# Up products of the first 512 tokens as float16 pairs, and five plain float32 down blocks, in a fused attention and two-network kernel

## The chip, the core and the metric

One core of a Trainium2 chip runs the whole program. The metric is the device time of one launch in microseconds. The kernel before was timed three times; the median is the number to compare with.

## What is computed

```python
# q, k, v: 2 x 8 x 768 x 64; proj: 64 x 6
bucket(y) = sum over n of 2**n * (y @ proj > 0)[n]
scores = where(bucket(q) == bucket(k), q @ k.T / 8, -1e9)
attn = softmax(scores) @ v
x = attn, heads side by side           # 1536 tokens x 512
h = x @ w_in                           # 512 -> 2048
x = (h - tanh(h)) @ w_out              # 2048 -> 512
p = domain_probs / sum
out = sum over e of p[:, e] * (relu(x @ w1[e]) @ w2[e])   # 4 experts, 512 -> 1024 -> 512
```

The weights of the first network arrive as float64 and are turned into float32 on the chip.

## The kernel before

TensorE is fed numbers of few bits, so nearly every product is made three times, from a high and a low part of each factor: high by high, high by low, low by high. A part is float16 or, in some places, float32r (a float32 that TensorE reads rounded). Where an operand is split, ScalarE or VectorE writes the high part and VectorE or GpSimd writes the low part, the source less the high part. A plain float32 product needs no split.

The work in order: the attention of 16 heads (`weights`, `maxima`, `prep`), up to 241 us; the first network, up to about 480 us; the second network.

In the first network the tokens go in three chunks of 512 (c = 0, 1, 2) and the hidden units in 16 blocks of 128 (fb).

- Up products of chunk 0 (`network_up`): they run while heads of the second batch are still in the attention, because chunk 0 needs only the first batch. The chunk's transposed input `xp` lies in the space `xa`, a float32r pair of 2 x 512 words for each of four row blocks; the block's weights `wu` lie in `wp0`, split by `split`. Twelve products of 128x512 make a block (L329, in `up_steps`), issued in two pieces of UPN = 6. ScalarE then takes the tanh (L984), VectorE the difference (L985).
- The weights (`conv`): for each block the two halves of a float64 tile come by DMA into `raw`; VectorE shifts and masks (L791, L796), ScalarE scales the low words (L334), GpSimd adds (L799). i = 0 is the block of w_in, i = 1 that of w_out. The converted w_out block takes a place of the class `fo` or `fo2` (`out_of`).
- Chunks 1 and 2 go up together by seven products in place of eight (`moving1`, `up7`, `seven`): sums and differences of four transposed quarters are cut into float16 pairs `bx` (the tiles named `ab`), those of two w_in blocks into `ax` (the tiles `fc` and `xa`). Their products are L920.
- Down products (`network_down`): for chunk 0 the blocks in FULL = (0, 1, 2) are plain float32, four products of 128x512 each (L994, recorded as two each); the other blocks split `th` into `g` (the tiles `hp`) and w_out into `wd` (the tiles `wp`) as float32r pairs and run L316, 12 products a block.

Places: before, `fo` and `fo2` are empty during the attention. `switch` makes seven and three places when the attention's own tiles are released; six more `fo` places come from `xa` and `wp0` after the up products of chunk 0 (`after_c0`).

The order on every engine is fixed when the program is built. `Plan.order` walks a model clock; each operation has a priority p (low goes first), a cost, and one or several engines that may do it, and it starts when its inputs and a place for its output are ready. For float32r up pieces the model adds ENTRY when TensorE comes to them from something else. The table T holds the priorities: `up0` and `up` for the up products, `m1` for `moving1`, `d0` and `d0s` for the down blocks of chunk 0. The conversion of a w_out block has the priority of its down block less `c1`.

Of the kernel before, what the change touches and what calls it, by code (L numbers as in the profile page):

```python
# [7 lines left out]
F16 = mybir.dt.float16  # L8
F32 = mybir.dt.float32
F32R = mybir.dt.float32r  # L10
U32 = mybir.dt.uint32
AF = mybir.ActivationFunctionType
# [40 lines left out]
WSI, XSI = 64.0, 4.0  # L53
GR = 2
TAIL = 3
FULL = (0, 1, 2)
FULL_ROWS = 0.86
ENTRY = 0.15
UPN = 6
WHOLE = ((1,), ())  # L60
PV32 = 1.3
EXPO = 0x7F800000
# [1 line left out]
NRQ = 2  # L64
TE, AC, VE, GP, DM_Q = "TE", "AC", "VE", "GP", "DQ"
T = dict(
    lead=10.23, lag=4.92, ahead=7.54, cut=3.18, up0=57.54, up=3.1, pre=23.64, bits=14.11, val=10.87,
    near=0.06, wait=20.39, slow=0.64, near0=0.004, begin=16.219, dma=0.65, done=0.9, hold=0.33,
    st0=129.04, sb0=-110.12, turn=228.92, near2=0.0, hold2=0.16, slow2=0.58, st=49.91, sb=31.04, dl=53.23, gs=79.64, bs=40.55, ns=7.06, ta=15.94,
    u7=358.17, u7s=22.26, d0=204.19, d0s=20.59, d1=408.55, d1s=13.63, m1=204.38, few=16, rest=295.92, cut7=25.22, cut70=142.27, g=13.58, c1=6.0, keep=0.0, x2=706.74, p0=746.54,  # L70
)


# [41 lines left out]
class Plan:  # L115
# [140 lines left out]
def attn_moe_kernel(ctx: ExitStack, tc: tile.TileContext, qk, v, proj, ident, wa, wb, dp, out):  # L256
# [11 lines left out]
    def space(name, words, kind=F32):  # L268
        if name not in places:
            places[name] = pool(name, 1)  # L270
        return places[name].tile([P, words], kind, name=name)
# [3 lines left out]

    rw_t, tp_t = space("rw", 2 * 2 * CH, U32), space("tp", NTH * CH)
    hp_t, hp2_t = space("hp", 2 * 2 * CH, F32R), space("hp2", 4 * CH)
    xa_t, wu_t = space("xa", KB4 * 2 * CH, F32R), space("wp0", 2 * 2 * CH, F32R)

    id32 = cp.tile([P, P], F32, name="id32")  # L280
    id16 = cp.tile([P, P], F16, name="id16")
# [18 lines left out]
    def part(t, at, n):  # L300
        return t[:, at : at + n]

    def pairs(t, at, n):
        return [part(t, at + 2 * CH * i, 2 * CH).rearrange("p (a b) -> p a b", a=2) for i in range(n)]

    def singles(t, at, n):
        return [part(t, at + CH * i, CH) for i in range(n)]
# [39 lines left out]
    def banks(n, name, shape=(P, CH)):  # L347
# [19 lines left out]
        den=tiles(2, [P, NB, 1], F32, "den"),  # L367

        f=singles(fa_t, 0, 14) + singles(fa2_t, 0, 2),
        fo=[],  # L370
        fo2=[],
        raw=raws(rw_t),
        wu=pairs(wu_t, 0, 2),
        wd=[],

        xp=pairs(xa_t, 0, KB4),
        g=pairs(hp_t, 0, 2),
        th=singles(tp_t, 0, NTH),
        th0=singles(hp2_t, 0, 4),
# [394 lines left out]
    w1 = {}  # L774

    def out_of(fb):
        return ("fo2" if fb < 3 else "fo", fb)

    def conv(fb, i, p):

# [21 lines left out]
    def split(p, dst, src, r, w, use=(), psum=False, gp=True, after=()):  # L802

        hi, lo = (lambda: dst()[:, 0, :]), (lambda: dst()[:, 1, :])
        how = {AC: (0.48 if psum else 0.52, act_copy(hi, src))}
        if not psum:
            how[VE] = (0.34, lambda: nc.vector.tensor_copy(hi(), src()))
        first = add(p, how, r, [(w, "hi")], use, port=not psum, after=after)
        h32 = lambda: hi().bitcast(F32)
        how = {VE: (0.6, sub(nc.vector, lo, src, h32))}  # L810
        if gp and not psum:
            how[GP] = (1.23, sub(nc.gpsimd, lo, src, h32))
        add(p + 0.1, how, [*r, (w, "hi")], [(w, "lo")], use, port=not psum)
        begun[w] = first
        return [(w, "hi"), (w, "lo")]
# [17 lines left out]
    def make_xT(c, kb, p):  # L833

        t = ("xp", c, kb)
        pt = turned(c, kb, p, [t])
        split(p + 0.1, lambda: pl[t], lambda: pl[pt], [pt], ("xT", c, kb), [t], psum=True)

    def scaled(p, hi, lo, src, by, n, r, k, use, psum=False):
        add(p, {AC: (0.05 + n * 0.92e-3, act_copy(hi, src, scale=by))}, r, [(k, "hi")], use)  # L840
# [128 lines left out]
    def network_up(c, fb, p, cut):  # L969

        w, ph, th = ("wu", c, fb), ("up", c, fb), th_of(c, fb)
        ks = split(p - cut, lambda: pl[w], lambda: pl["f", fb], [("f", fb)], ("w", c, fb, 0), [w])
        steps = {}

        def step(m):
            if not m:
                steps.update(enumerate(up_steps(pl[ph], pl[w], [pl["xp", c, kb] for kb in range(KB4)])))
            steps[m]()

        for m in range(0, 3 * KB4, UPN):  # L980
            add(p, {TE: (0.227 * UPN, lambda m=m: [step(m + i) for i in range(UPN)])},
                ks + [(("xT", c, kb), i) for kb in range(KB4) for i in ("hi", "lo")], [ph],
                [w] + [("xp", c, kb) for kb in range(KB4)], run="up")
        add(p + 0.5, {AC: (0.48, lambda: nc.scalar.activation(pl[th], pl[ph], AF.Tanh, scale=1.0 / XSI))}, [ph], [th])  # L984
        add(p + 0.6, {VE: (0.6, lambda: nc.vector.scalar_tensor_tensor(  # L985
            out=pl[th], in0=pl[ph], scalar=1.0 / XSI, in1=pl[th], op0=ALU.mult, op1=ALU.subtract
        ))}, [ph, th], [th])

    def network_down(c, fb, p, cut):
# [404 lines left out]
    for fb in range(NF1):  # L1394
        conv(fb, 0, up_at(fb) - T["ahead"])
    for fb in range(NF1):
        conv(fb, 1, down_at(0, fb) - T["c1"])
    for fb in range(NF1):
        network_up(0, fb, up_at(fb), T["cut"])
    moving1(T["m1"])  # L1400
# [117 lines left out]
    c0 = those("xp", "wu")  # L1518

    def after_c0():  # L1520
        t = late["xa"] = space("xa", 8 * CH)
        late.update(ax=sevens(t, 0), fo=singles(t, 7 * CH // 2, 4))
        t = space("wp0", 4 * CH)
        late["sx"] = quads(t, 0)
        late["fo"] += singles(t, 2 * CH, 2)
        return late["fo"]

    gives_later("fo", 6, after_c0, c0)
    gives_later("ax", 1, lambda: late["ax"], c0)
    gives_later("wr", 2, lambda: made["th1"], those("th1"))  # L1530
    gives_later("sx", 1, lambda: late["sx"], c0)
    gives_later("g", 2, lambda: pairs(space("hp2", 4 * CH, F32R), 0, 2), those("th0"))
# [107 lines left out]
```

## Time and profile before

| what | before |
|---|---|
| median of 3 runs | 914.13 us (913.98 to 917.42) |
| the profiled execution | 916.71 us |
| its span, first to last instruction | 914.9 us |
| TensorE (PE) busy | 893.8 us, 98% |
| VectorE (DVE) busy | 799.5 us, 87% |
| ScalarE (ACT) busy | 630.9 us, 69% |
| GpSimd (POOL) busy | 428.0 us, 47% |
| mean granted TensorE clock | 0.994 |

Busy time is the time in which at least one instruction of the engine is in flight. Matmuls overlap, so the spacing of their starts, not their duration, says what one costs.

### The profile page before, as it was taken

How to read it: one execution, taken by the hardware profiler on the slowest of the kernel's cores; microseconds unless marked ns; L12 is line 12 of the kernel's file. 1: busy time of each engine (PE TensorE's matmuls, PEld its weight loads, DVE VectorE, ACT ScalarE, POOL GpSimd, SP SyncE). 2: the span in 40 equal slices, each digit the busy share in tenths (PEclk: the TensorE clock that was granted, in tenths of full speed). 3: DMA queues.
4: the chain of work that ended last, by engine and by line, in shares of the span. 5: the costliest groups of instructions: out<-in, count | busy, mean ns of one | idle time of the engine just before them, and what ended most of it. 6: DMA issues, size and time to landing. Idle time of an engine off the chain costs nothing.

```text
span 914.9 us, 19244 instructions
## 1 busy us (share of the span) xinstructions
PE 893.8 (98%) x7206; PEld 642.6 (70%) x7206; DVE 799.5 (87%) x1518; ACT 630.9 (69%) x1356; POOL 428.0 (47%) x448
## 2 busy tenths in 40 slices
PE   8999999999969999999999999999999999999997
PEld 3777777777736555768866777777777777777777
DVE  7988889898898897669898989989998989989785
ACT  7898998888655765335478876676765756666562
POOL 4687867877552342102024435655254543534322
PEclk8999999999999999999999999999999999999999
DMA  6534443222413100011000110111010111100003
GB/s 173 142 88 109 110 109 104 68 87 73 139 62 123 70 24 0 1 47 47 24 12 13 58 36 25 47 47 48 28 67 12 47 37 47 47 24 24 2 1 138
DMA packets 43283, 53.90 MB, mean 59 GB/s; under 512 B 18422, under 2 KB 23350, under 8 KB 43190
## 3 DMA queue, kind: packets, MB, share of 16 engines
q1 hardware_dynamic: 43190, 52.68, 18.8%
q8 instruction: 56, 0.92, 0.4%
q14 instruction: 37, 0.30, 0.1%
HBM read 43.18 MB, written 3.15 MB: 51 GB/s over the span
## 4 chain that ended last, share of the span: by engine, by line
PE 89%; DVE 6%; ACT 3%; DMA 1%; issue 1%; SPq 1%; POOL 0%; DVEq 0%; ACTq 0%; POOLq 0%
PE st L1223 13%; PE po L1132 9%; PE sf L1223 9%; PE sf L1132 8%; PE sf L316 7%; PE st L316 7%; PE st L1132 5%; PE sf L329 5%; PE st L665 4%; PE sf L578 3%; PE st L670 3%; PE po L920 3%; PE st L920 2%; PE sf L920 2%; PE po L725 2%; PE po L724 2%
## 5 line engine op out<-in xcount | busy, mean ns | idle before, releaser
L337 POOL TENSOR_TENSOR ph<-p,ph 128x384 f16<-128x384 f32 x122 | 117.7, 984 | 52.6 <-ACT ph L676 31.9
L584 DVE TENSOR_REDUCE mx<-sf 128x1 f32<-128x384 f32 x192 | 99.0, 549 | 13.2 <-PE sf L578 11.9
L1223 PEld LDWEIGHTS <-fb 128*128 128x128 f16 x999 | 97.7, 98 | 13.8 <-issue 0.4
L676 ACT ACTIVATE ph<-st 128x384 f16<-128x384 f32 x176 | 86.0, 510 | 0.7 <-PE st L670 0.4
L676 ACT ACTIVATE p<-st 128x384 f32<-128x384 f32 x144 | 72.1, 506 | 8.9 <-PE st L670 7.2
L316 PE MATMUL sf<-hp,wp 128*128 128x512 f32 x270 | 71.8, 401 | 0.0
L1132 PEld LDWEIGHTS <-ab 128*128 128x128 f16 x504 | 49.1, 98 | 32.1 <-issue 2.8
L316 PE MATMUL st<-hp,wp 128*128 128x512 f32 x270 | 69.1, 390 | 0.0
L665 PE MATMUL st<-qk 97*128 97x384 f16 x192 | 63.9, 333 | 2.7 <-DVE bt L501 1.1
L670 PE MATMUL st<-qk 128*128 128x384 f16 x192 | 63.9, 333 | 0.0
L337 POOL TENSOR_TENSOR fb<-tp,fb 128x384 f16<-128x384 f32 x32 | 32.5, 1022 | 59.6 <-ACT fb L1168 59.6
L316 PEld LDWEIGHTS sf<-hp,wp 128*128 128x128 f32 x270 | 50.6, 188 | 11.8
L1132 PEld LDWEIGHTS <-fc 128*128 128x128 f16 x420 | 41.1, 98 | 25.0
L1132 PEld LDWEIGHTS <-tp 128*128 128x128 f16 x420 | 41.1, 98 | 24.6
L316 PEld LDWEIGHTS st<-hp,wp 128*128 128x128 f32 x270 | 50.7, 188 | 10.9
L578 PE MATMUL sf<-qk 96*128 96x384 f16 x192 | 55.9, 329 | 1.2 <-DMA qk<-bt 1.0
L724 PE MATMUL po<-v,ph 128*128 128x65 f16 x528 | 56.9, 193 | 0.0
L725 PE MATMUL po<-v,ph 128*128 128x64 f16 x528 | 56.9, 195 | 0.0
L1223 PEld LDWEIGHTS <-wp 128*128 128x128 f16 x513 | 50.2, 98 | 9.5 <-issue 0.3
L726 PE MATMUL po<-v,ph 128*128 128x65 f16 x528 | 56.7, 191 | 0.0
L1223 PE MATMUL st<-rw,fb 128*128 128x256 f16 x345 | 56.5, 273 | 0.0
L1223 PEld LDWEIGHTS <-xa 128*128 128x128 f16 x504 | 49.3, 98 | 10.0 <-issue 1.8
(473 smaller groups left out, 2674.3 us busy)
## 6 DMA issues: line engine op xcount, KB each, us to landing
rw<-wa SPq DMA_DIRECT2D x48, 256.0 KB
ab<-wb SPq DMA_DIRECT2D x32, 256.0 KB
xa<-wb SPq DMA_DIRECT2D x32, 256.0 KB
r<-qk SPq DMA_DIRECT2D x15, 384.0 KB
qk<-qk SPq DMA_DIRECT2D x58, 96.0 KB
rq<-wa SPq DMA_DIRECT2D x16, 256.0 KB
vr<-v SPq DMA_DIRECT2D x8, 384.0 KB
out<-xs SPq DMA_DIRECT2D x12, 256.0 KB
```

The lines of the kernel that those rows point to most:

```text
L316: nc.tensor.matmul(acc, a, g[:, i, :], start=(first and n == 0), stop=(last and n == 2))
L337: return lambda: eng.tensor_tensor(out=dst(), in0=a(), in1=b(), op=ALU.subtract)
L578: nc.tensor.matmul(pl[ps][:, 0:384], t[0:96, QA, qt * P : qt * P + P], t[0:96, KB, j * 384 : j * 384 + 384], start=True, stop=True,)
L584: nc.vector.tensor_reduce(out=pl["mx", h][:, qt, j : j + 1], in_=pl[ps][:, 0:384], axis=AX.X, op=ALU.max)
L665: nc.tensor.matmul(ps[j][:, 0:384], t[0:97, KB, kt * P : kt * P + P], t[0:97, QA, j * 384 : j * 384 + 384], start=True, stop=False,)
L670: nc.tensor.matmul(ps[j][:, 0:384], t[:, KC, kt * P : kt * P + P], t[:, QC, j * 384 : j * 384 + 384], start=False, stop=True,)
L676: nc.scalar.activation(o.rearrange("p (a b) -> p a b", a=2)[:, js[0]], pl[st][:, 0:384], AF.Exp, scale=1.0 / (8.0 * SC * SC), **kw)
L724: nc.tensor.matmul(o[:, c : c + D + 1], hi, vt[:, kt, 0 : D + 1], start=(kt == 0 and qt == 0), stop=False)
L725: nc.tensor.matmul(o[:, c : c + D], hi, vt[:, kt, D + 1 : 2 * D + 1], start=False, stop=False)
L920: nc.tensor.matmul(pl[x], s, pl["bx", o][:, k, i, :], start=(first and k == 0 and n == 0), stop=(k == 1 and n == 2), skip_group_check=True,)
L1132: nc.tensor.matmul(bank(x), s, pl["bo%d" % b, o][:, k, i, :], start=(first and n == 0), stop=(n == 5), skip_group_check=True)
L1223: nc.tensor.matmul(pl[x][:, 256 * t : 256 * t + 256], y, pl["bb", u][:, w, i, :], start=(first and n == 0), stop=(n == 3 * nt * GR - 1), s ...
```

## The change

1. `network_up` makes its operands as float16 pairs: `xp` and `wu` take half the words, the weights are scaled by WSI = 64 as they are cut, and the tanh undoes the scale. The high part may be written by ScalarE or VectorE as before; the low part is now VectorE's alone (before: VectorE or GpSimd). The twelve products are issued one by one (UPN = 1), without a group for the planner.
2. The words freed in `xa` and `wp0` are six `fo` places that exist from the start.
3. FULL has five blocks. Their w_out blocks go to `fo` (`fo2` now takes blocks 6, 7, 8), are converted at priority `cf` + `cfs` fb, and the blocks run at `df` + `dfs` fb. `moving1` has 215 for 204.38.
4. Other numbers of T move a little (`lag`, `ahead`, `pre`, `near`, `cut7`, `x2`, `p0`, `ta` and others).

```diff
-FULL = (0, 1, 2)
+FO2 = (6, 7, 8)
+FULL = (0,1,2,3,4)
-UPN = 6
+UPN = 1
...
-    u7=358.17, u7s=22.26, d0=204.19, d0s=20.59, d1=408.55, d1s=13.63, m1=204.38, few=16, rest=295.92, cut7=25.22, cut70=142.27, g=13.58, c1=6.0, keep=0.0, x2=706.74, p0=746.54,
+    u7=357.98, u7s=22.91, d0=204.19, d0s=20.59, d1=408.55, d1s=14.1, m1=215.0, few=16, rest=296.19, cut7=26.6, cut70=138.0, g=13.58, c1=6.0, keep=0.0, df=230.0, dfs=3.0, cf=190.0, cfs=8.51, x2=700.61, p0=751.67,
...
-    xa_t, wu_t = space("xa", KB4 * 2 * CH, F32R), space("wp0", 2 * 2 * CH, F32R)
+    xa_t, wu_t = space("xa", 8 * CH), space("wp0", 4 * CH)
+    def pairs16(t, at, n):
+        return [part(t, at + CH * i, CH).bitcast(F16).rearrange("p (a b) -> p a b", a=2) for i in range(n)]
-        fo=[],
+        fo=singles(xa_t, 4 * CH, 4) + singles(wu_t, 2 * CH, 2),
-        wu=pairs(wu_t, 0, 2),
+        wu=pairs16(wu_t, 0, 2),
-        xp=pairs(xa_t, 0, KB4),
+        xp=pairs16(xa_t, 0, KB4),
-        return ("fo2" if fb < 3 else "fo", fb)
+        return ("fo2" if fb in FO2 else "fo", fb)
     def network_up(c, fb, p, cut):
-        ks = split(p - cut, lambda: pl[w], lambda: pl["f", fb], [("f", fb)], ("w", c, fb, 0), [w])
+        key, src, hi, lo = ("w", c, fb, 0), (lambda: pl["f", fb]), (lambda: pl[w][:, 0]), (lambda: pl[w][:, 1])
+        add(p - cut, {AC: (0.52, act_copy(hi, src, scale=WSI)), VE: (0.34, lambda: nc.vector.tensor_scalar(
+            out=hi(), in0=src(), scalar1=WSI, scalar2=None, op0=ALU.mult
+        ))}, [("f", fb)], [(key, "hi")], [w], port=True)
+        add(p - cut + 0.1, {VE: (0.6, lambda: nc.vector.scalar_tensor_tensor(
+            out=lo(), in0=src(), scalar=WSI, in1=hi(), op0=ALU.mult, op1=ALU.subtract
+        ))}, [("f", fb), (key, "hi")], [(key, "lo")], [w], port=True)
+        ks = [(key, "hi"), (key, "lo")]
-            add(p, {TE: (0.227 * UPN, lambda m=m: [step(m + i) for i in range(UPN)])},
-                [w] + [("xp", c, kb) for kb in range(KB4)], run="up")
+            add(p, {TE: (0.2145 * UPN, lambda m=m: [step(m + i) for i in range(UPN)])},
+                [w] + [("xp", c, kb) for kb in range(KB4)])
     def down_at(c, fb):
+        if c == 0 and fb in FULL:
+            return T["df"] + T["dfs"] * fb
-        conv(fb, 1, down_at(0, fb) - T["c1"])
+        conv(fb, 1, T["cf"] + T["cfs"] * fb if fb in FULL else down_at(0, fb) - T["c1"])
     def after_c0():
-        t = late["xa"] = space("xa", 8 * CH)
-        late.update(ax=sevens(t, 0), fo=singles(t, 7 * CH // 2, 4))
-        t = space("wp0", 4 * CH)
-        late["sx"] = quads(t, 0)
-        late["fo"] += singles(t, 2 * CH, 2)
-        return late["fo"]
-    gives_later("fo", 6, after_c0, c0)
-    gives_later("ax", 1, lambda: late["ax"], c0)
+        late.update(xa=xa_t, sx=quads(wu_t, 0))
+        return sevens(xa_t, 0)
+    gives_later("ax", 1, after_c0, c0)
```

How the order moves, at two places. In the changed kernel the line numbers are 4 to 13 higher: L333 is the old L329, L831 the old L827, L1007 the old L994, L926 the old L920.

TensorE just after the attention, before: the transposes of chunks 1 and 2 (L827), plain float32 blocks (L994), and the first seven-way product (L920).

```order
L827 MATMUL sf_152<-id_93,xs_102 128x128 x4
L827 MATMUL po_154<-id_93,xs_102 128x128 x4
L827 MATMUL po_155<-id_93,xs_103 128x128 x4
L994 MATMUL sf_151<-hp_84,fb_4337 128x512
L994 MATMUL sf_153<-hp_84,fb_4337 128x512
L827 MATMUL po_155<-id_93,xs_103 128x128 x4
L827 MATMUL st_148<-id_93,xs_102 128x128 x4
L994 MATMUL st_149<-hp_84,fb_4337 128x512
L994 MATMUL st_150<-hp_84,fb_4337 128x512
L920 LDWEIGHTS fc
L920 MATMUL sf_152<-ab,fc 128x512
```

The same place in the change (w_out blocks now in `xa`, `wp` and `fb`):

```order
L1007 MATMUL st_150<-hp_84,wp_92 128x512
L1007 MATMUL st_148<-hp_84,wp_92 128x512
L1007 MATMUL sf_151<-hp_84,fb 128x512
L1007 MATMUL sf_153<-hp_84,fb 128x512
L1007 MATMUL st_150<-hp_84,fb 128x512
L1007 MATMUL st_148<-hp_84,fb 128x512
L1007 MATMUL sf_151<-tp,fb 128x512
L1007 MATMUL sf_153<-tp,fb 128x512
L1007 MATMUL st_150<-tp,fb 128x512
L1007 MATMUL st_148<-tp,fb 128x512
L926 LDWEIGHTS fc
L926 MATMUL po_154<-ab,fc 128x512
```

Before, two plain float32 blocks stand ahead of the first L920 product and the third behind 39 of them; now all five, 20 products, stand ahead of the first, and the first float32r down product follows 39 seven-way products later (before: 42).

VectorE in the last head of the attention, before: low halves of the softmax weights (L337 and L696 on `ph`), conversions of w_in (L791, L796), tanh differences (L985).

```order
L337 TENSOR_TENSOR ph_142<-p_0_138,ph_142 128x384
L791 TENSOR_SCALAR fa<-rw 128x512
L796 SCALAR_TENSOR_TENSOR fa<-rw,fa 128x512
L337 TENSOR_TENSOR ph_143<-p_1_139,ph_143 128x384
L696 TENSOR_TENSOR ph_144<-st_148,ph_144 128x384
L696 TENSOR_TENSOR ph_144<-st_149,ph_144 128x384
L985 SCALAR_TENSOR_TENSOR tp<-sf_152,tp 128x512
L791 TENSOR_SCALAR fa_68<-rw 128x512
L337 TENSOR_TENSOR ph_145<-p_2_140,ph_145 128x384
```

The same place in the change (L341 is the old L337, L700 the old L696, L998 the old L985; L982 is the new low half of w_in):

```order
L341 TENSOR_TENSOR ph_142<-p_0_138,ph_142 128x384 x2
L795 TENSOR_SCALAR fa<-rw 128x512
L341 TENSOR_TENSOR ph_143<-p_1_139,ph_143 128x384
L800 SCALAR_TENSOR_TENSOR fa<-rw,fa 128x512
L341 TENSOR_TENSOR ph_143<-p_1_139,ph_143 128x384
L979 TENSOR_SCALAR wp_92<-fa 128x512
L700 TENSOR_TENSOR ph_144<-st_148,ph_144 128x384
L700 TENSOR_TENSOR ph_144<-st_150,ph_144 128x384
L998 SCALAR_TENSOR_TENSOR tp<-sf_152,tp 128x512
L982 SCALAR_TENSOR_TENSOR wp_92<-fa,wp_92 128x512
L341 TENSOR_TENSOR ph_145<-p_2_140,ph_145 128x384
L982 SCALAR_TENSOR_TENSOR wp_92<-fa,wp_92 128x512
```

Both low halves of a softmax block are VectorE's here where GpSimd had one, and two low halves of w_in have come in.

## Rows read from the trace of the kernel before

**Rows 1.** The page, busy time of each engine.

```profile
PE 893.8 (98%) x7206; PEld 642.6 (70%) x7206; DVE 799.5 (87%) x1518; ACT 630.9 (69%) x1356; POOL 428.0 (47%) x448
```

**Rows 2.** Windows: length, PE, PEld, DVE, ACT, POOL busy, clock, DMA, GB/s.

```profile
41.50:241.50 200.00, 198.16 (x2558) 146.35 (x2557) 176.38 (x369) 177.79 (x421) 153.20 (x163) 1.00 0.33 93
173.00:190.00 17.00, 17.00 (x193) 12.10 (x192) 16.31 (x34) 15.19 (x36) 14.28 (x15) 1.00 0.28 79
241.50:279.60 38.10, 30.82 (x121) 16.80 (x122) 36.26 (x57) 20.65 (x38) 19.30 (x17) 0.96 0.36 121
560.00:600.00 40.00, 38.33 (x295) 28.55 (x293) 38.60 (x73) 24.15 (x54) 22.08 (x23) 1.00 0.11 34
```

**Rows 3.** Waits of VectorE, 41.5 to 241.5 us: total, times, longest.

```profile
DVE mx L584 <- PE sf L578: 10.6, 29, 1.1
```

**Rows 4.** Timeline of TensorE in the attention: start, duration, instructions.

```profile
151.70 0.34 PE L665 MATMUL st<-qk 97*128 97x384 f16 x1
...
152.04 0.49 PE L578 MATMUL sf<-qk 96*128 96x384 f16 x2
152.23 1.69 PE L329 MATMUL sf<-xa,wp 128*128 128x512 f32 x6
153.75 0.34 PE L665 MATMUL st<-qk 97*128 97x384 f16 x1
```

**Rows 5.** Timeline of TensorE from the attention's end, at 241.36 us.

```profile
241.36 3.06 PE L329 MATMUL st<-xa,wp 128*128 128x512 f32 x12
244.25 2.89 PE L329 MATMUL sf<-xa,wp 128*128 128x512 f32 x12
246.98 0.60 PE L827 MATMUL po<-id,xs 128*128 128x128 f32 x4
247.41 1.88 PE L994 MATMUL sf<-hp,fb 128*128 128x512 f32 x4
249.13 1.88 PE L994 MATMUL st<-hp,fb 128*128 128x512 f32 x4
...
258.40 1.46 PE L920 MATMUL sf<-ab,fc 128*128 128x512 f16 x6
259.69 0.81 PE L920 MATMUL po<-ab,fc 128*128 128x512 f16 x3
...
273.47 1.44 PE L920 MATMUL sf<-ab,xa 128*128 128x512 f16 x3 [3.46 <-DVE fa L939]
274.70 2.92 PE L994 MATMUL sf<-hp,fb 128*128 128x512 f32 x4
...
279.63 1.75 PE L316 MATMUL sf<-hp,wp 128*128 128x512 f32 x6
```

**Rows 6.** Groups by line and form, 41.5 to 241.5 us: count, busy, mean ns.

```profile
L337 DVE TENSOR_TENSOR ph<-p,ph 128x384 f16<-128x384 f32 x22 | 15.4, 698 | 4.2 <-ACT ph L676 4.0
L337 DVE TENSOR_TENSOR wp<-fa,wp 128x512 fp32r<-128x512 f32 x6 | 4.7, 784 | 0.8 <-ACT wp L334 0.8
...
L337 POOL TENSOR_TENSOR ph<-p,ph 128x384 f16<-128x384 f32 x109 | 104.9, 983 | 33.9 <-ACT ph L676 16.0 <-PE po L726 5.9 <-PE sf L578 4.3
```

**Rows 7.** Timeline of VectorE after its last instruction of the attention.

```profile
242.43 0.42 DVE L791 TENSOR_SCALAR fb<-rw 128x512 uint32<-128x512 uint32 x1
...
243.11 0.68 DVE L796 SCALAR_TENSOR_TENSOR fb<-rw,fb 128x512 uint32<-128x512 uint32 x1
243.71 0.41 DVE L895 TENSOR_TENSOR fc<-fc,fa 128x256 f32<-128x256 f32 x1
244.04 1.53 DVE L895 TENSOR_TENSOR fc<-fa 128x256 f32<-128x256 f32 x1
...
267.71 1.21 DVE L841 SCALAR_TENSOR_TENSOR xa<-wp,xa 128x1024 f16<-128x1024 f32 x1
268.84 0.41 DVE L791 TENSOR_SCALAR xa<-rq 128x512 uint32<-128x512 uint32 x1
...
277.51 0.68 DVE L337 TENSOR_TENSOR wp<-xa,wp 128x512 fp32r<-128x512 f32 x1
```

More of the change, by code (lines that the diff above doesn't have):

```diff
@@ L66 @@
 T = dict(
-    lead=10.23, lag=4.92, ahead=7.54, cut=3.18, up0=57.54, up=3.1, pre=23.64, bits=14.11, val=10.87,
-    near=0.06, wait=20.39, slow=0.64, near0=0.004, begin=16.219, dma=0.65, done=0.9, hold=0.33,
-    st0=129.04, sb0=-110.12, turn=228.92, near2=0.0, hold2=0.16, slow2=0.58, st=49.91, sb=31.04, dl=53.23, gs=79.64, bs=40.55, ns=7.06, ta=15.94,
-    u7=358.17, u7s=22.26, d0=204.19, d0s=20.59, d1=408.55, d1s=13.63, m1=204.38, few=16, rest=295.92, cut7=25.22, cut70=142.27, g=13.58, c1=6.0, keep=0.0, x2=706.74, p0=746.54,
+    lead=10.23, lag=5.23, ahead=7.72, cut=3.22, up0=57.54, up=3.1, pre=23.46, bits=14.11, val=10.87,
+    near=0.0, wait=20.39, slow=0.64, near0=0.004, begin=16.219, dma=0.65, done=0.9, hold=0.33,
+    st0=129.04, sb0=-114.08, turn=224.83, near2=0.0, hold2=0.16, slow2=0.58, st=49.91, sb=31.04, dl=53.23, gs=79.64, bs=40.55, ns=7.15, ta=16.93,
+    u7=357.98, u7s=22.91, d0=204.19, d0s=20.59, d1=408.55, d1s=14.1, m1=215.0, few=16, rest=296.19, cut7=26.6, cut70=138.0, g=13.58, c1=6.0, keep=0.0, df=230.0, dfs=3.0, cf=190.0, cfs=8.51, x2=700.61, p0=751.67,
 )
@@ L836, in make_xT @@
         pt = turned(c, kb, p, [t])
-        split(p + 0.1, lambda: pl[t], lambda: pl[pt], [pt], ("xT", c, kb), [t], psum=True)
+        x, hi, lo, key = (lambda: pl[pt]), (lambda: pl[t][:, 0]), (lambda: pl[t][:, 1]), ("xT", c, kb)
+        add(p + 0.1, {AC: (0.48, act_copy(hi, x))}, [pt], [(key, "hi")], [t])
+        add(p + 0.2, {VE: (0.6, sub(nc.vector, lo, x, hi))}, [pt, (key, "hi")], [(key, "lo")], [t])
     def scaled(p, hi, lo, src, by, n, r, k, use, psum=False):
@@ L980, in network_up @@
         for m in range(0, 3 * KB4, UPN):
-            add(p, {TE: (0.227 * UPN, lambda m=m: [step(m + i) for i in range(UPN)])},
+            add(p, {TE: (0.2145 * UPN, lambda m=m: [step(m + i) for i in range(UPN)])},
                 ks + [(("xT", c, kb), i) for kb in range(KB4) for i in ("hi", "lo")], [ph],
-                [w] + [("xp", c, kb) for kb in range(KB4)], run="up")
-        add(p + 0.5, {AC: (0.48, lambda: nc.scalar.activation(pl[th], pl[ph], AF.Tanh, scale=1.0 / XSI))}, [ph], [th])
+                [w] + [("xp", c, kb) for kb in range(KB4)])
+        add(p + 0.5, {AC: (0.48, lambda: nc.scalar.activation(pl[th], pl[ph], AF.Tanh, scale=1.0 / (WSI * XSI)))}, [ph], [th])
         add(p + 0.6, {VE: (0.6, lambda: nc.vector.scalar_tensor_tensor(
-            out=pl[th], in0=pl[ph], scalar=1.0 / XSI, in1=pl[th], op0=ALU.mult, op1=ALU.subtract
+            out=pl[th], in0=pl[ph], scalar=1.0 / (WSI * XSI), in1=pl[th], op0=ALU.mult, op1=ALU.subtract
         ))}, [ph, th], [th])
```

## The prediction

> **What bounds the kernel now.** I read the page first, then windows, waits and timelines. On the page TensorE is busy 98% of the span, VectorE 87% [rows 1]. So a change pays if it takes work from TensorE or fills its gaps, and it costs if another engine falls behind in a stretch that has no room.
>
> The windows show where each is the case. In the attention with up products (41.5 to 241.5 us) TensorE is busy for 198.2 of 200 us, VectorE for 176.4 [rows 2]. The largest wait of VectorE there is for TensorE's scores, 10.6 of its 23.6 us of idle time [rows 3]: TensorE is the bound and VectorE has 12% to spare. From 241.5 to 279.6 it is the other way: VectorE is busy 36.3 of 38.1 us, TensorE 30.8, and the granted clock is 0.96 [rows 2]. There TensorE waits for sums, cuts and weight conversions that stand in one queue on VectorE; the longest wait is 3.46 us, and after it three products take 1.23 us where three take 0.65, so they ran at the lower of the clock's two levels, half speed [rows 5].
>
> **The change part by part.**
>
> *Up products as float16.* The second dozen after the attention starts at 244.25 and ends where the next begins, 246.98: 2.73 us, 0.2275 each, in float32r. Six float16 products of the same 128x512 go from 258.40 to 259.69, 0.215 each [rows 5]. 192 products times 0.0125 is 2.4 us. Coming to float32r from float16 may cost something as well: the first dozen took 2.89, 0.16 more [rows 5], but in mid attention two score products and six up products take 1.71 us (152.04 to 153.75), of which two such score products are 0.34 and the six 1.365, so nearly nothing [rows 4]. Before there are 25 such runs; I take 0.06 each, since most runs stand between score products, 1.5 us (ends 0.2 and 4.0). Sum: **-3.9 us** (-2.6 to -6.4). The change has 47 shorter runs, but with the type of their neighbours. Twice the weight loads hide as they do for the seven-way products, which run at 0.215 with them.
>
> *Two more plain float32 blocks.* Four rows from 247.41 to 249.13 are two products, so 0.86 each [rows 5]. Eight more are 6.9 us; 24 float32r products at 0.2275 go, 5.5 us. Four more changes of kind among the down blocks (22 for 18) at 0.06 are 0.2. Sum: **+1.6 us**. The splits of two blocks go with them: work of VectorE, ScalarE and GpSimd that costs nothing while TensorE is the bound, and so saves nothing either.
>
> *The stretch behind the attention.* From 241.36 to the first float32r down product at 279.63 are 38.3 us [rows 5]. In them stand 24 up products (5.6 with the entry), 8 groups of transposes at 0.43 (3.4), 12 plain float32 products (10.3) and 42 seven-way products (9.0): 28.4 us. So 9.9 us are lost to waits and to the slow clock after them. In the change, between the same two points, stand 24 float16 up products (5.2), the same transposes (3.4), 20 plain products (17.2) and 39 seven-way ones (8.4): 34.2 us. The five blocks are work that needs only w_out and old tanh differences, so they cover VectorE while it makes the sums.
>
> Do they cover it? VectorE issues 49 instructions from 242.43 to 277.51, where the low half for the first down product begins. 33 of 512 wide at 0.60, 14 narrow ones at 0.33 and 2 of 1024 at 1.13 would be 26.8 us; they took 35.1 [rows 7]. The other 8.3 us are a few instructions like the one at 244.04 that takes 1.53 in place of 0.41, each while GpSimd is at work. In the change the same queue, up to the same low half, has 35, 14 and 2 of these kinds and the four small ones on `dsum` that moved here: 28.7 us. With 8.3 us lost again, and 1.07 from 241.36 to 242.43, TensorE could start its first down product at 38.2 us and loses 4.0; with none lost it loses nothing. GpSimd has 13 instructions in the stretch, before 14, so I take a loss near the first end, 3.0. Sum: **-6.9 us** (-5.9 to -9.9). The conversions have their places from the start, but the order puts all but the first step of the first one behind the attention; their loads, two a block, are queued behind those of the last heads as before, so the queue of loads moves nothing on the path.
>
> *VectorE in the attention.* What is late next is here. Up to the last head's output VectorE has 15 low halves of w_in where it had 6, and 31 low halves of softmax weights where it had 22, because GpSimd may no longer cut w_in and the planner spread the rest anew. At their mean durations, 0.784 and 0.698 [rows 6], 18 more are 13.3 us: 189.7 of the 196.5 us that TensorE still needs there (200 less 3.5 of the up saving), 96.5%. Two rows say what that costs. From 173 to 190 VectorE is busy 96% and TensorE loses nothing; from 560 to 600 it is busy 96.5% and TensorE loses 1.7 of 40 us [rows 2], which is 8.2 for 196.5. The first is the same kind of work, so I take **+1.5 us** (0 to 8.2).
>
> *The rest* (lower `lag`, `ahead`, second network) moves priorities, not work; I take 0.
>
> Sum: -3.9 + 1.6 - 6.9 + 1.5 = -7.7 us. The profiled execution took 916.7 us, 2.6 above the median of the runs shown; like it the change would take 909.0, and as a median 914.1 - 7.7 = **906.4 us**. All good ends give 899.4, all bad ones 915.4.
>
> **The rivals.**
>
> *VectorE meets GpSimd at every moved instruction.* The rows of VectorE's low halves are means over meeting and not meeting GpSimd. If each of the 18 waited for a whole GpSimd instruction, 0.983 us [rows 6], VectorE would have 17.7 us more, 207.4, more than TensorE's 196.5: +10.9 in place of +1.5, and 915.8 us. For it: 1.53 for 0.41 at 244.04 [rows 7]. Against it: GpSimd was busy 153 of 200 us [rows 2] and gives up 18 instructions, and the mean of 698 ns leaves no room for a wait of 983 each time. This is what the Trainium skill states (SBUF — State Buffer, Who interferes with whom): a VectorE instruction with two SBUF inputs and a GpSimd instruction that reads SBUF exclude each other, and the later one blocks for the whole of the other. At its worst, with a GpSimd instruction in the way each time, that rule gives this rival's time; the row at 244.04 agrees with it, the mean of 698 ns does not agree with its worst.
>
> *VectorE's idle time is latency, not room.* If the 23.6 us of idle time stay as they are, because a chain from score to maximum to exponential sets them, the attention becomes 189.7 + 23.6 = 213.3 us: +16.8 in place of +1.5, and **921.7 us, slower**. It ends above the old time from +9.2 on, that is if more than 16.0 of the 23.6 us stay. For it: 13 us of the waits are not for scores. Against: the largest are for scores that a busy TensorE had not yet issued [rows 3].
>
> *No loss in either place.* GpSimd's lighter load frees VectorE, the queue behind the attention runs at its plain spacing: -3.9 + 1.6 - 9.9 = 901.9 us.
>
> *The float16 products gain nothing in place,* because their weight loads do not hide between short attention products. Then the first term is 0 and the time 910.3. Against: six seven-way products in a row with their loads at 0.215 [rows 5].
>
> **How the numbers follow.** Forecast 0.66, no loss 0.15, GpSimd met each time 0.08, latency 0.06, no gain in place 0.05. A measurement of this kernel tells about 0.5% from no change, 909.6 to 918.7 us. The forecast's own ends (loss in the attention up to 5, behind it up to 4) reach 911, so some 0.57 of its 0.66 are faster; with 0.15 and 0.02 that makes 0.74 faster. The remainder of the forecast, 0.08 and 0.03 are 0.20 the same; 0.06 slower. The range 900.5 to 912.0 holds the forecast, the case without loss and the one without gain in place; it leaves out the two cases of a late VectorE and the far end of the good one, 0.18.
>
> **What would show it.** Right: up products at 0.215 with no float32r among them before 241 us; VectorE at about 96% from 41.5 us to the attention's end, and that end some 2 us earlier; from there 34 to 38 us to the first float32r down product, with no wait over 2 us and a granted clock of 1.00. Wrong: waits of TensorE for VectorE's low halves of `ph` or `wp` that sum to more than 5 us in the attention, or a wait of some microseconds in front of the first seven-way products, which would say that five blocks do not cover the sums.

## The result and the profile after

The changed kernel takes **906.7 us** (median of 4 runs, 905.49 to 908.67), the kernel before beside it 915.77 us. The ratio is 0.9893 [0.9845, 0.9941]: faster by 1.1%. Two more samples on other chips gave 0.9909 [0.9888, 0.9931] and 0.9924 [0.9906, 0.9941]. The forecast was 906.4 us.

The program splits at three events that every trace has: the last step of the first head and of the last head (six products of 3x65), and the first product of the second network. Each entry is the time between two of them, read from TensorE's timeline to about 0.1 us.

| kernel | to the first head | attention | first network behind it | second network |
|---|---|---|---|---|
| before | 37.2 | 204.0 | 217.3 | 456.4 |
| the change | 36.7 | 203.3 | 209.3 | 455.2 |
| the change, second and third sample | 39.3, 39.0 | 204.0, 204.5 | 209.3, 209.3 | 455.3, 455.2 |
| `e1_f16_alone` | 36.8 | 201.9 | 215.6 | 456.5 |
| `e4_two_behind` | 37.1 | 203.0 | 215.4 | 455.2 |
| `e3_three_full` | 37.6 | 203.8 | 219.0 | 455.2 |
| `e7_six_full` | 37.5 | 203.2 | 209.1 | 455.3 |
| `e6_four_full` | 36.8 | 199.1 | 226.0 | 455.2 |
| `e5_gpsimd_cuts` | 37.1 | 205.3 | 212.4 | 455.2 |
| `e8_runs_of_six` | 37.2 | 191.9 | 234.0 | 455.2 |
| `e10_old_attention`, twice | 36.8, 36.1 | 202.0, 201.9 | 210.0, 210.0 | 455.3, 455.3 |

The first column is scatter: the same program gives 36.7 and 39.3. So kernels are compared here by the other three. The saving lies in one place: 8.0 us in the first network behind the attention, the same in three samples. Of these 8.0 us, 1.6 are a low granted clock in the one traced execution of the kernel before; that of `e1_f16_alone`, after the same wait, does not have it (shown there). The attention gains nothing on the mean (203.9 for 204.0), the second network 1.2. The attention of the change alone scatters by 1.2 us, so differences of about 1 us in that column say little.

The page of the change, busy time of each engine (before: [rows 1]):

```profile
PE 887.6 (98%) x7198; PEld 623.9 (69%) x7198; DVE 802.2 (89%) x1537; ACT 632.6 (70%) x1356; POOL 393.9 (44%) x421
```

The shares hardly moved, and do not show where the time went. The windows do (columns as in [rows 2]):

```profile
41.50:240.00 198.50, 195.58 (x2555) 132.88 (x2555) 182.60 (x381) 175.22 (x417) 128.51 (x144) 1.00 0.34 93
173.00:190.00 17.00, 16.51 (x211) 10.45 (x209) 15.29 (x32) 14.39 (x34) 10.59 (x12) 1.00 0.29 79
240.00:274.50 34.50, 34.43 (x140) 17.01 (x138) 34.05 (x63) 23.82 (x43) 16.73 (x13) 1.00 0.43 141
560.00:600.00 40.00, 40.00 (x300) 29.11 (x298) 36.99 (x72) 28.24 (x62) 15.91 (x17) 1.00 0.16 54
```

The third row answers to the third of [rows 2]. There TensorE was busy 30.82 of 38.10 us at a clock of 0.96; now it is busy 34.43 of 34.50 at 1.00. It does more work in less time, because it no longer stops and its clock no longer falls. VectorE is still busy for nearly all of the stretch (34.05), but TensorE no longer waits for it. The first row shows the price in the attention: GpSimd's busy time fell by 24.7 us (153.2 to 128.5), VectorE's rose by 6.2 (176.4 to 182.6).

TensorE's timeline from the attention's end (before: [rows 5]):

```profile
240.12 2.76 PE L333 MATMUL st<-xa,wp 128*128 128x512 f16 x12
242.72 0.60 PE L831 MATMUL sf<-id,xs 128*128 128x128 f32 x4
...
246.62 1.02 PE L1007 MATMUL sf<-hp,xa 128*128 128x512 f32 x2
...
259.41 1.88 PE L1007 MATMUL sf<-hp,fb 128*128 128x512 f32 x4
261.13 1.88 PE L1007 MATMUL st<-hp,fb 128*128 128x512 f32 x4
262.85 1.88 PE L1007 MATMUL sf<-tp,fb 128*128 128x512 f32 x4
264.56 1.88 PE L1007 MATMUL st<-tp,fb 128*128 128x512 f32 x4
266.28 2.75 PE L926 MATMUL po<-ab,fc 128*128 128x512 f16 x12
268.87 1.46 PE L926 MATMUL sf<-ab,fc 128*128 128x512 f16 x6
...
274.09 0.81 PE L926 MATMUL st<-ab,xa 128*128 128x512 f16 x3
274.55 1.74 PE L320 MATMUL sf<-hp,wp 128*128 128x512 f32 x6
```

Not one row of the stretch has an idle time in brackets. Twelve float16 up products take 242.72 - 240.12 = 2.60 us, 0.217 each. From 240.12 to the first float32r down product (L320) are 34.4 us, for 34.2 us of work as the prediction counted it. Before it was 38.3 for 28.4. The first seven-way product (L926) comes 26.2 us into the stretch, before 17.0 us. That is the mechanism: ahead of it TensorE has 25.8 us of work that needs only old inputs, before 15.9 (with two plain blocks in place of five), and when it reaches the sums they are there.

VectorE in the same stretch (before: [rows 7]), two rows that are longer than their kind (243.04 and 270.94), others that are not, and the low half for the first down product (273.61):

```profile
243.04 1.85 DVE L901 TENSOR_TENSOR fc<-fa 128x256 f32<-128x256 f32 x2
...
247.09 0.41 DVE L901 TENSOR_TENSOR fc<-fa,fc 128x256 f32<-128x256 f32 x1
...
252.04 0.68 DVE L341 TENSOR_TENSOR ab<-xa,ab 128x512 f16<-128x512 f32 x1
252.65 0.68 DVE L800 SCALAR_TENSOR_TENSOR fb<-rq,fb 128x512 uint32<-128x512 uint32 x1
253.25 0.68 DVE L341 TENSOR_TENSOR ab<-wp,ab 128x512 f16<-128x512 f32 x1
253.85 0.68 DVE L341 TENSOR_TENSOR ab<-st,ab 128x512 f16<-128x512 f32 x1
...
264.23 1.29 DVE L341 TENSOR_TENSOR ab<-fb,ab 128x512 f16<-128x512 f32 x2 [0.19 <-ACT ab L338]
...
270.94 1.80 DVE L341 TENSOR_TENSOR hp<-tp,hp 128x512 fp32r<-128x512 f32 x1
...
273.61 0.68 DVE L341 TENSOR_TENSOR wp<-xa,wp 128x512 fp32r<-128x512 f32 x1
```

From 241.84, the answer to 242.43 before, to 273.61 are 31.8 us for the 28.7 that the prediction summed: 3.1 us lost to long instructions, before 8.3. And GpSimd's timeline in the same stretch:

```profile
251.92 3.17 POOL L803 TENSOR_TENSOR wp<-wp,rq 128x512 uint32<-128x512 uint32 x1 [0.80 <-ACT ab L338]
255.05 1.30 POOL L803 TENSOR_TENSOR fb<-fb,rq 128x512 uint32<-128x512 uint32 x1
258.92 2.16 POOL L803 TENSOR_TENSOR fb<-fb,rw 128x512 uint32<-128x512 uint32 x1 [2.57 <-issue]
```

Two of these adds take 3.17 and 2.16 us where their kind takes 1.30, beside a VectorE that runs at its plain spacing. Here it is GpSimd that is held up; before it was VectorE (1.53 for 0.41 at 244.04 [rows 7]). Beside the add of 3.17 us VectorE runs three instructions in a row that read two SBUF tiles (252.04, 252.65, 253.25). The next one, at 253.85, reads a sum of TensorE (`st`) and one SBUF tile, and from its start to the add's end at 255.09 are 1.24 us, about the plain length of the add. So by these rows GpSimd was held through three instructions, not one.

In the attention, the low halves by group (before: [rows 6]):

```profile
L341 POOL TENSOR_TENSOR ph<-p,ph 128x384 f16<-128x384 f32 x99 | 93.5, 963 | 38.5 <-ACT ph L680 17.3 <-issue 7.4 <-PE st L674 4.2
...
L341 DVE TENSOR_TENSOR ph<-p,ph 128x384 f16<-128x384 f32 x31 | 22.3, 741 | 0.9 <-ACT ph L680 0.9
L982 DVE SCALAR_TENSOR_TENSOR wp<-fa,wp 128x512 f16<-128x512 f32 x15 | 10.3, 684 | 0.2
```

The counts are the predicted 31 and 15. VectorE's wait for scores, 10.6 us in [rows 3], is still its largest:

```profile
DVE mx L588 <- PE sf L582: 8.4, 14, 1.7
```

So TensorE is still the bound there, with less margin.

### The profile page after: what moved, and what is told of

It is laid out like the page before. It is cut to its first block, busy times and chain, and to the rows that moved or that the text cites. A ratio compares the mean times of both kernels' runs of the same rounds, so it can differ in the third digit from the quotient of the medians.

```text
span 904.5 us, 19207 instructions
## 1 busy us (share of the span) xinstructions
PE 887.6 (98%) x7198; PEld 623.9 (69%) x7198; DVE 802.2 (89%) x1537; ACT 632.6 (70%) x1356; POOL 393.9 (44%) x421
## 4 chain that ended last, share of the span: by engine, by line
PE 87%; DVE 5%; DMA 3%; ACT 3%; issue 1%; SPq 1%; POOL 0%; DVEq 0%; ACTq 0%
PE st L1236 14%; PE po L1145 9%; PE sf L1236 9%; PE sf L1145 9%; PE sf L320 7%; PE st L320 6%; PE st L1145 4%; PE po L926 4%; PE sf L333 4%; PE st L669 3%; PE st L674 2%; PE sf L582 2%; PE sf L926 2%; PE st L926 2%; PE po L729 1%; PE po L728 1%
## 5 line engine op out<-in xcount | busy, mean ns | idle before, releaser
L341 POOL TENSOR_TENSOR ph<-p,ph 128x384 f16<-128x384 f32 x113 | 106.8, 964 | 57.4 <-ACT ph L680 35.9
L1264 DVE SCALAR_TENSOR_TENSOR xs<-st,pw,xs 128x256 f32<-128x256 f32 x132 | 59.5, 477 | 14.9 <-PE st L1236 13.2
L320 PE MATMUL sf<-hp,wp 128*128 128x512 f32 x258 | 70.0, 405 | 0.0
L338 ACT ACTIVATE hp<-sf,pw 128x256 f32<-128x256 f32 x96 | 41.3, 474 | 36.2 <-PE sf L1236 35.4
L320 PE MATMUL st<-hp,wp 128*128 128x512 f32 x258 | 66.4, 391 | 0.0
L320 PEld LDWEIGHTS sf<-hp,wp 128*128 128x128 f32 x258 | 48.3, 188 | 11.6 <-DVE wp L341 0.2
L320 PEld LDWEIGHTS st<-hp,wp 128*128 128x128 f32 x258 | 48.5, 188 | 10.5
```

Of the source, the lines that this page charges most:

```text
L320: nc.tensor.matmul(acc, a, g[:, i, :], start=(first and n == 0), stop=(last and n == 2))
L341: return lambda: eng.tensor_tensor(out=dst(), in0=a(), in1=b(), op=ALU.subtract)
```

## The experiments

**Theory.** The saving is cover: five plain float32 blocks, whose inputs are old, stand where TensorE waited for VectorE's sums. Float16 gives 0.0125 us a product and little else; VectorE's extra low halves cost the attention 1 to 2 us. **Rivals.** The saving is float16 itself (rate, or dearer entries into float32r than thought); or it is the splits that two more plain blocks save, wherever these stand; or it is the planner's new order and not the blocks.

### a1_change and a2_change: the change again, on two other chips

No edit.

> The change itself, beside the experiments on one chip. From the first timing: ratio 0.989 to the kernel before, and in the profile 34.4 us from the last head's end (240.1 us) to the first float32r down product. Both theories expect that again.

Measured: 907.54 us, 0.9909 [0.9888, 0.9931].

> The changed kernel again, on one chip with the two runs beside it: 0.989 to 0.991 of the time before.

Measured: 909.85 us, 0.9924 [0.9906, 0.9941]. Both samples lie above the first, and their starts are 2.3 to 2.6 us later; behind the attention all three read 209.3.

### e1_f16_alone: only the up operands as float16

The kernel before with `xp` and `wu` as float16 pairs, everything else and its order untouched:

```diff
-    xa_t, wu_t = space("xa", KB4 * 2 * CH, F32R), space("wp0", 2 * 2 * CH, F32R)
+    xa_t, wu_t = space("xa", KB4 * 2 * CH), space("wp0", 2 * 2 * CH)
...
-        wu=pairs(wu_t, 0, 2),
+        wu=pairs16(wu_t, 0, 2),
...
-        xp=pairs(xa_t, 0, KB4),
+        xp=pairs16(xa_t, 0, KB4),
```

> The kernel before with one thing changed: the up products of the first 512 tokens are float16 pairs; every instruction stands in the order of before. Theory P (the prediction's term: rate and a cost of coming to float32r of 0.06 us): 3.9 us faster, attention's end 3.5 us earlier. Theory Q (rate alone, 0.0125 us a product, entry costs nothing): 2.4 us faster, attention's end 2.1 us earlier than 241.4. Both: the stretch behind the attention still loses 8 to 10 us.

Measured: 914.18 us, 0.9978 [0.9964, 0.9992], so -0.7 to -3.3 us. The attention is 201.9 us, 2.1 less than before, which is what the rate alone gives for its 168 products. But TensorE's waits in it are 0.5 us longer here (2.3 for 1.8), so the products themselves gave more. The place of [rows 4] in this run:

```profile
151.35 0.49 PE L581 MATMUL sf<-qk 96*128 96x384 f16 x2
151.68 1.46 PE L332 MATMUL sf<-xa,wp 128*128 128x512 f16 x6
152.97 0.33 PE L668 MATMUL st<-qk 97*128 97x384 f16 x1
```

From the two scores to the product behind the piece are 1.62 us, where [rows 4] has 1.71; 0.075 of the 0.09 is the rate. Read in this way, the 23 pieces of the attention with like neighbours in both runs (162 products) save 2.72 us, 0.70 more than the rate gives: 0.03 us a piece. The 24 products behind the attention take 5.20 us for the 5.62 of [rows 5], 0.12 more than the rate. So coming to float32r from float16 costs about 0.03 us, half of the 0.06 that theory P took.

TensorE's waits from 238 to 276 us:

```profile
PE sf L923 <- DVE fa L942: 3.5, 1, 3.5
PE po L923 <- DVE ab L340: 1.4, 1, 1.4
PE po L830 <- DVE fb L340: 1.3, 1, 1.3
PE st L923 <- ACT fa L337: 1.1, 1, 1.1
```

These are the waits of before, in the same place; the longest answers to the 3.46 us of [rows 5]. What differs is the clock after it. From the first product behind that wait to the first float32r down product, the same work before and here (columns as in [rows 2]):

```profile
273.47:279.63 6.16, 6.16 (x15) 2.66 (x14) 4.71 (x8) 1.94 (x5) 1.28 (x1) 0.73 0.72 235
270.96:275.50 4.54, 4.54 (x15) 2.03 (x14) 4.54 (x8) 1.94 (x5) 1.28 (x1) 1.00 0.82 243
```

That is 1.6 of the 1.7 us by which this kernel is shorter behind the attention (215.6 for 217.3). So the same wait is followed by a low clock in one execution and by the full one in another. So float16 is worth about a quarter of the gain and leaves the stops behind the attention as they were; beside this run, with the full clock, the change still saves 6.3 us there (209.3 for 215.6).

### e4_two_behind: two of the five blocks behind the first seven-way products

The change, with the fourth and fifth plain block held back until the first seven products of each sum have been issued:

```diff
+    behind = []
...
+        if u == 0:
+            behind.append(pl.ops[-1])
...
-                ))}, [out_of(fb), th], [("acc", c, db)])
+                ))}, [out_of(fb), th], [("acc", c, db)], after=behind if fb > 2 else ())
```

> The change, but the fourth and fifth plain float32 blocks may start only behind the seven products of the first two w_in blocks: the same products, the same splits, other places. Cover theory (the blocks fill TensorE's wait for VectorE): TensorE waits 4 to 7 us before or among the first seven-way products again and the time is 4 to 7 us above the change, 911 to 914. Rival (two blocks fewer to split relieve VectorE, wherever they stand): within 1.5 us of the change.

Measured: 913.13 us, 0.997 [0.9954, 0.9985], 5.6 us above the change on the same chip. TensorE's work is the same, five plain blocks and no split more. TensorE's timeline:

```profile
266.67 1.04 PE L928 MATMUL st<-ab,xa 128*128 128x512 f16 x4 [0.97 <-DVE xa L847]
268.39 1.46 PE L928 MATMUL st<-ab,xa 128*128 128x512 f16 x6 [0.69 <-ACT fa L338]
271.82 0.81 PE L928 MATMUL po<-ab,xa 128*128 128x512 f16 x3 [1.97 <-DVE fa L947]
272.46 2.09 PE L928 MATMUL po<-ab,fc 128*128 128x512 f16 x6
274.35 2.56 PE L928 MATMUL sf<-ab,fc 128*128 128x512 f16 x6
276.74 1.46 PE L928 MATMUL po<-ab,fc 128*128 128x512 f16 x6
```

and the window with the two slow rows:

```profile
272.40:276.80 4.40, 4.40 (x15) 1.67 (x13) 4.40 (x8) 1.72 (x3) 1.84 (x2) 0.61 0.67 230
```

The waits are back, 3.6 us in three rows. After them the granted clock is 0.61 on the mean of 4.4 us, between the clock's two levels of 1.2 and 2.4 GHz, though TensorE is busy throughout: twelve products from 272.46 to 276.74 take 4.28 us where twelve at 0.215 take 2.58, so 1.7 more. 3.6 + 1.7 = 5.3 of the 5.6 us. This run tells cover from saved splits, and the splits fall: the two blocks' own saving is still in it, and it is 5.6 us slower.

### e3_three_full, e6_four_full, e7_six_full: how many blocks

One line of the change each, for `FULL = (0,1,2,3,4)`:

```diff
+FULL = (0,1,2)
...
+FULL = (0,1,2,3)
...
+FULL = (0,1,2,3,4,5)
```

> The change with FULL = (0, 1, 2), all else left: float16 up products and early places stay, two blocks go back to float32r pairs. Cover theory: 6.9 us of TensorE's work is missing behind the attention, VectorE's queue is not shorter, so TensorE waits 4 to 7 us there; 1.4 us of product time is saved; the sum is 3 to 5.5 us above the change, 910.5 to 913. Rival (the gain is the float16 products and the early places): within 1.5 us of the change, or faster by the 1.4 us.

Measured: 918.21 us, 1.0021 [1.0007, 1.0034], slower than the kernel before. The direction is the expected one, the size is not: behind the attention it takes 219.0 us, 9.7 more than the change. Its longest waits from 241 to 282 us, and the window in which they lie:

```profile
PE sf L926 <- DVE fa L945: 3.8, 1, 3.8
PE sf L926 <- DVE ab L341: 1.5, 1, 1.5
```

```profile
259.00:281.00 22.00, 16.37 (x54) 6.66 (x54) 20.69 (x33) 10.52 (x18) 8.31 (x6) 0.84 0.28 95
```

The wait of 3.5 us for the `fa` of [rows 5] is here again, 3.8 us long, with a clock of 0.84 over 22 us. The size adds up from more than the cover theory priced: 6.3 us of waits in the stretch, one more wait of 2.3 us behind it, and 15 products after the longest wait (275.45 to 281.10) that take 5.65 us where 15 at 0.215 take 3.2. Less the 1.4 us of product time and the 0.4 us that the change waits behind the stretch too, that is 9.2 of the 9.7. With all the change's other edits but three plain blocks for five, all of the gain is lost. But e1 has three blocks too and takes 215.6 us there, so 3.4 of the 9.7 belong to this order, whose numbers were chosen for five blocks, and to the low clock in it.

> The change with six plain float32 blocks, which is all the early places hold. Cover theory: five already cover the wait, so the sixth only costs its 0.7 us: +0.3 to +1.2 us beside the change, no wait behind the attention. Rival (each block fewer to split relieves VectorE): 1 to 2 us faster than the change.

Measured: 907.42 us, 0.9915 [0.9884, 0.9945], 209.1 us behind the attention, with no wait from 240.5 to 279 us. A sixth block has nothing left to cover, as expected.

> The change with four plain float32 blocks. TensorE would come to the first seven-way product 22.9 us after the last head, where the change takes 26.3; VectorE's last cut of the quarter sums came 25.3 us after it in the change. Cover theory: a wait of 0 to 2.5 us, 0.7 us of product time saved, so -0.7 to +2 us beside the change. Rival (lighter splits): +0 to +2 too, but without a wait before the seven-way products.

Measured: 919.97 us, 1.0043 [1.0015, 1.007]. A miss, and no test of four blocks: with four, the planner leaves eight dozens of up products behind the last head where the change leaves two, and the first seven-way product comes 38.9 us after it (the change: 26.3). The attention is only 4 to 5 us shorter for six dozens less, 15.5 us of products.

### e5_gpsimd_cuts: GpSimd may cut w_in again

The change with the old cut of the weights:

```diff
-        add(p - cut + 0.1, {VE: (0.6, lambda: nc.vector.scalar_tensor_tensor(
-            out=lo(), in0=src(), scalar=WSI, in1=hi(), op0=ALU.mult, op1=ALU.subtract
-        ))}, [("f", fb), (key, "hi")], [(key, "lo")], [w], port=True)
+        add(p - cut + 0.1, {VE: (0.6, sub(nc.vector, lo, src, hi)), GP: (1.23, sub(nc.gpsimd, lo, src, hi))}, [("f", fb), (key, "hi")], [(key, "lo")], [w], port=True)
```

> The change, but GpSimd may again write the low half of w_in, and the planner gives it 7 of 16 or so (weights unscaled, so that both engines do the same subtraction). If VectorE's 18 more instructions in the attention cost what was predicted, 1.5 us: 0.5 to 1.5 us faster. If VectorE there is the bound (rival with GpSimd met each time): 3 to 9 us faster. If nothing: within 0.5 us.

Measured: 914.11 us, 0.9982 [0.9969, 0.9996], 6.6 above the change on the same chip: a miss. The whole order was planned anew around it. In the attention (205.3 us) TensorE waits longest for something that has nothing to do with the cuts, a transfer:

```profile
PE st L669 <- DMA qk<-mt: 2.2, 3, 1.3
```

and behind it 2.1 us for a cut of VectorE (`ab`). The run says that a small edit can make the planner write an order that is 6 us worse; it does not say what VectorE's cuts cost.

### e8_runs_of_six: up products six at a time

```diff
-UPN = 1
+UPN = 6
```

> The change with up products planned six at a time in place of one at a time, GpSimd still barred from the cuts of w_in. If the extra low halves on VectorE are the cost, the attention stays at 203 to 204 us and the time within 0.5 us of the change; if the fine pieces are (scores that come later, more changes of kind), the attention falls to about 202 us and the time by 1 to 2 us.

Measured: 922.33 us, 1.0065 [1.0045, 1.0085], 12.5 above the change on the same chip. Both theories missed. (The pieces of six are not kept together as a group here, as they were before.) Windows of its attention and of the stretch behind it:

```profile
41.50:229.00 187.50, 178.12 (x2451) 124.94 (x2450) 172.28 (x369) 165.17 (x400) 124.36 (x140) 0.99 0.35 99
229.00:280.40 51.40, 49.23 (x208) 23.43 (x207) 51.04 (x85) 32.52 (x59) 24.99 (x17) 1.00 0.34 113
```

The planner put eleven of the sixteen dozens behind the last head. Without nine dozens (23.2 us of products) the attention is only 12 us shorter, and TensorE is idle for 9.4 of 187.5 us in it, where it was 2.9 of 198.5. Behind the attention it is 24.7 us longer. So in the attention the up products are fill as well: in this order about half of the time of those that left comes back. The other half is what this kernel loses.

### e10_old_attention: the five early blocks with the attention of before

Both edits at once, cuts as in e5 and pieces as in e8, and with them the numbers that the kernel before had for its attention:

```diff
-UPN = 1
+UPN = 6
...
-    lead=10.23, lag=5.23, ahead=7.72, cut=3.22, up0=57.54, up=3.1, pre=23.46, bits=14.11, val=10.87,
-    near=0.0, wait=20.39, slow=0.64, near0=0.004, begin=16.219, dma=0.65, done=0.9, hold=0.33,
+    lead=10.23, lag=4.92, ahead=7.54, cut=3.18, up0=57.54, up=3.1, pre=23.64, bits=14.11, val=10.87,
+    near=0.06, wait=20.39, slow=0.64, near0=0.004, begin=16.219, dma=0.65, done=0.9, hold=0.33,
...
-            add(p, {TE: (0.2145 * UPN, lambda m=m: [step(m + i) for i in range(UPN)])},
-                [w] + [("xp", c, kb) for kb in range(KB4)])
+            add(p, {TE: (0.227 * UPN, lambda m=m: [step(m + i) for i in range(UPN)])},
+                [w] + [("xp", c, kb) for kb in range(KB4)], run="up")
```

> The change with the attention planned as before (six up products to a piece, the old lags, GpSimd may cut w_in) and the five early blocks kept. If VectorE's 18 more instructions cost the change its attention time: the attention takes 202 us from the first head's end to the last, as in float16 alone, not 203.3 to 204, and the stretch behind it is as in the change: 1.5 to 2 us faster, 905 to 906 beside 907.5. Rival (GpSimd's cuts of w_in are late for the conversions that follow, as where it cut them in the change's own plan): 2 to 7 us slower than the change.

Measured: 905.64 us (904.84 to 905.88), 0.9876 [0.9855, 0.9896]. Once more, beside the change on one chip:

> The five early blocks with the cuts and the order of the attention of before, once more. If VectorE's extra low halves cost the change what its attention is longer (203.3 us against 202.0), this run is 1 to 2 us below the change on the same chip, ratio 0.987 to 0.989; if the one earlier run was chance, the two are equal within 0.5 us.

Measured: 905.95 us against the change's 909.85; ratios 0.9891 [0.9866, 0.9916] and 0.9924 [0.9906, 0.9941]. It beats the kernel before, and both its medians lie below all three of the change (906.7 to 909.85); the intervals of the two still touch. The attention is 201.9 us for 204.5, the stretch behind it 0.7 longer: 1.9 us of the 3.9 by stages. The rest is the earlier start (36.1 for 39.0), which is scatter. The attention by windows, the change's third sample first, then this kernel:

```profile
41.50:243.50 202.00, 197.83 (x2583) 134.27 (x2582) 184.65 (x386) 178.31 (x423) 131.30 (x147) 1.00 0.33 93
```

```profile
41.50:238.00 196.50, 194.13 (x2549) 132.34 (x2548) 177.00 (x365) 176.19 (x418) 149.99 (x161) 1.00 0.33 94
```

VectorE is busy 90% here and 91.4% there. With the five early blocks kept, the attention is back at the 201.9 us of e1. So what the change pays in the attention is not the price of the early blocks. Whether it is VectorE's low halves or the single pieces is open: the two runs that took one away at a time moved much else.

## Why the prediction was right

The forecast was 906.4 for 906.7 us. That they lie 0.3 us apart is in part luck. The forecast starts from 914.1 us for the kernel before, which took 915.8 beside the change, so the medians differ by 9.1 us where 7.7 were forecast. And by steps, errors of both signs stand against each other. What was right is the mechanism of the likeliest case: the saving is the cover behind the attention.

*Up products as float16, -3.9.* The rate was right: 0.217 by the timeline, and 0.215 in e1. Too high was "I take 0.06 each" for 25 entries into float32r: e1 shows about 0.03, 0.8 us in place of 1.5. The products themselves gave some 3.2 us; about 0.5 of that went into longer waits of e1's attention, and what reached the time is 2.1 us there and 0.4 behind it: the term is -2.5. The [rows 4] that the prediction set aside, nearly nothing in mid attention, were the better witness.

*Two more plain blocks, +1.6.* Nothing contradicts it. From the first float32r down product to the second network it is 174.8 us where it was 178.9: 4.1 less. By the prediction's rows it would be 4.6 (24 float32r products less, three seven-way ones and four changes of kind more), and TensorE waits 0.4 us there.

*The stretch behind the attention, -6.9.* The mechanism is right: e4 takes the cover away with all work kept and loses 5.6 us. The step "I take a loss near the first end, 3.0" failed: TensorE lost 0.2, so the term is -9.7. The prediction carried over 8.3 us of long VectorE instructions; there were 3.1. Its own model, 28.7 + 1.07 + 3.1 and 0.68 for the last low half, which it had left out, ends at 33.6 us, before TensorE's 34.2 us of work are done. So next to nothing was lost. The second end of its range was the truth. But of the 9.9 us that it found lost before, 1.6 are the low clock of that one execution; beside an execution like e1's the term is -8 to -9.

*VectorE in the attention, +1.5.* The three samples of the change take 203.3 to 204.5 us, e1 201.9 without the moved cuts: 1.4 to 2.6. The size is right, the reading of the load is not. Eighteen more low halves came as counted, and as long as forecast: 31 x 0.741 and 15 x 0.684, less the 22 x 0.698 and 6 x 0.784 of [rows 6], are 13.2 us. But VectorE is busy for 182.6 of 198.5 us, 92% and not 96.5%: busy time rose by 6.2 us, not 13.3. The prediction added durations to a busy time in which instructions overlap; those at 252.04 and 252.65 above start 0.61 us apart and last 0.68. And VectorE has 12 more instructions there and not 18: four of those that are gone are the small ones on `dsum`, 1.7 us, which the prediction itself had placed behind the attention. That the extra time is VectorE's load is argued, not shown. TensorE's named waits in the attention rise from 1.8 to 2.6, 3.7 and 3.8 us, but only 0.3, 1.1 and 1.1 of these are for low halves of `ph`, and e1, with a shorter attention than any of them, has 2.3. Two of the signs that the prediction named are therefore wrong: VectorE at 96%, and an attention that ends 2 us earlier. The other signs (0.215 a product, 34 to 38 us, no long wait, a clock of 1.00) came as named.

*The rest, 0.* The second network became 1.2 us shorter, in every kernel with the new numbers and not in e1 (456.5). That points to the numbers for its order, which the prediction set at nothing.

Sum of the terms as measured: -2.5 + 1.6 - 9.7 + 2.0 - 1.2 = -9.8 us, against -7.7 forecast. The three ratios times 915.8 us give -9.8, -8.3 and -7.0, each uncertain by 1.6 to 4.4.

*The rivals.* VectorE held up by GpSimd each time: the means, 741 and 684 ns, exclude it, and behind the attention it was often GpSimd that was held up. This is what the Trainium skill says (SBUF — State Buffer, Who interferes with whom): the one that issues second is blocked, whichever it is. The rows of both traces agree, 1.53 us on VectorE before and 3.17 us on GpSimd after, where it was held through three instructions in a row. VectorE's idle time as latency: it fell from 23.6 to 15.9 us, so most of what was added went into room. But e6 and e8, whose attention shortens by only a third to a half of the up products that leave it, say that the rival was nearer than it was taken to be: below 202 us TensorE is no longer the only bound of the attention. No loss in either place was half right, behind the attention and not in it. No gain of float16 in place: in e1 six products between attention products take 1.29 us (151.68 to 152.97), 0.215 each, which excludes it.

## What to carry to other kernels

Where a bound engine meets a stretch of dependent work of another engine, look for work whose inputs are long ready and put it there, even in a dearer form: 0.86 us of a plain float32 product for the 0.68 of the three split ones that it replaces bought a stretch without stops. Stop when the stretch is covered; the sixth block gave nothing. That the early places of the blocks' inputs were needed is argued; no run has the five blocks without them. Judge a change by stages between events that both traces have: here the start of the program alone scatters by 3 us, a third of the gain.

## What was not expected of the hardware

- A stop can cost more than its length, but not each time. In e4, 3.6 us of waits in three rows were followed by 4.4 us at a granted clock of 0.61, 1.7 us more; in e3 the clock was 0.84 over 22 us. After the same wait of 3.46 us the kernel before ran 6.16 us at 0.73, and e1 did that work in 4.54 us at 1.00. In the change, with no wait, the clock is 1.00 throughout the stretch.
- The meeting of VectorE and GpSimd lengthens now one and now the other: the same kind of add took 1.30 and 3.17 us on GpSimd. A sum of durations from one trace does not carry over to another order: 8.3 us lost before, 3.1 after, for nearly the same queue.
- Going from float16 products to float32r has a small price, about 0.03 us a time in the attention by e1, and 0.16 us in the first dozen of [rows 5] beside the second.
